# A mixture of experts on one core: each rank gets its own narrow width, six more second products branch, two ranks change the way their second products run

## The chip, the cores and the metric

The kernel runs on one core of a Trainium2 chip. The metric is the device time of one execution in microseconds (us), as the median of several runs. TensorE is called PE here, VectorE DVE, ScalarE ACT, GpSimd POOL and SyncE SP.

## What is computed

Clustered attention over 4 batches, 8 heads and 768 positions makes 3072 tokens of 512 numbers. Then a mixture of experts with 16 experts runs on them. Each token goes to one expert, the best of the best group:

```
for g in range(G):
    ...
    for e in range(Eg):
        ...
        h = np.maximum(xg[mask_e] @ w1[g, e], 0.0)
        ye = h @ w2[g, e]
        combined = g_w[mask_g][mask_e] * e_w[mask_e]
        tok_idx = np.where(mask_g)[0][mask_e]
        out[tok_idx] = combined[:, None] * ye
```

The first products (`@ w1`) take 512 features to 1024, the second ones (`@ w2`) take them back to 512. The change touches only the mixture of experts.

## The kernel before, in words

**Stages.** Attention runs to about 392 us. The first expert and the leftover tokens follow (`part_a`, `bridge`), and from 436 us on the other 15 experts, in falling order of their number of tokens, which the kernel finds at run time. Such a place in the order is called a rank, 0 to 14. A rank has a fixed capacity, the widest it may be: `caps` = 288, 272, 256, 240, 232, 224, 216, 208, 200, 192, 184, 176, 168, 160, 160 tokens. With this input (the reference's own, from its fixed seed) the reference's routing gives the ranks 271, 234, 213, 207, 191, 189, 178, 177, 174, 169, 155, 142, 142, 141 and 133 tokens.

**A round** (`round_`, from L1450). Round k holds the first products of rank k (`up`, L1029) and the second products of rank k-1 (`down`, L1056), taken in turn over eight steps. Every value is carried as a sum of two float16 numbers, a high and a low part, so each product of matrices is made three times (high by high, high by low, low by high).

**First products.** `up` makes 8 accumulations of 12 products (L1044), two accumulations to a step, 96 products of M columns in a rank, M being the rank's capacity or less. Their eviction is one ACT instruction for the high part (`hh`, L1049) and one DVE instruction for the low part (`hl`, L1050) per accumulation.

**Second products, in one of two ways.** By features, `down` makes 4 pieces of 24 products of M columns each (L1078) and evicts each piece by ACT (`yh`, L1084) and DVE (`yl`, L1085). One round on, `settle` turns the result back to tokens with 8 products of 128 columns for each tile of 128 tokens (L1128). By tokens, it makes 24 products of 512 columns for each tile of 128 tokens (L1102), however many tokens the tile has, and no turning back is needed. `feature_major` (L1108) picks the way whose sum of columns is smaller: with M tokens in nt tiles it is by features if 96M + 1024nt < 12288nt. Ranks 2 and 3 go by tokens before the change, the others by features. Either way, each tile's result is scaled by ACT (L1141) and written out by an indirect DMA from POOL's queue (L1142).

**Narrow widths.** `widths` (L1249) compares each rank's count with its capacity and makes a word `wi` with one bit for each rank. `at_width` (L1273) wraps a run of products in a branch on PE: the bit chooses between a body of full width and one that is narrower by `STEP` = 24 columns. The first product of each accumulation has the full width in both bodies. Only the products change, and evictions keep the full width. The first products of all 15 ranks branch; of the second products by features only those of ranks below `CHOSEN` = 9 do. Those in a branch are 24 products in one piece, the others two pieces of 12.

**The stream of weights** (`stream`, L977). Each round brings 8 chunks of 512 KB (`load_chunk`, issued by SP, L818). A chunk's high part is made by ACT (L825) or POOL (L827) in turn, its low part by DVE (L828). These conversions stand at fixed places in the engines' queues between the evictions, since the order of PE, ACT and DVE is that of the program text here (`manual_schedule`). Two sets of weight tiles take turns: rank k+2's weights go into the tiles of rank k. In round 2 the stream has come to the first two chunks of rank 3's second weights by the last steps, and they go into the tiles that rank 1's second products read.

Of the kernel before, what the change touches and what calls it, by code (L numbers as in the profile page):

```python
# [744 lines left out]
class Experts:  # L745
# [11 lines left out]
    TURNED, TURN = (3, 4, 6, 8, 14), 3  # L757
    HI = (0, 1, 0, 1, 0, 1, 0, 1)
    LEAD = 12
    STEP, CHOSEN, BOUND = 24, 9, 15  # L760

    def __init__(self, ctx, tc, R, w1, w2, out, stage, wa):
        self.tc, self.R, self.w1, self.w2, self.out = tc, R, w1, w2, out
# [16 lines left out]
    def setup(self):  # L780
        nc, const, E = self.nc, self.const, self.R.E
        self.io = const.tile([P, E], F32, name="io")
        nc.gpsimd.iota(self.io, [[1, E]], base=0, channel_multiplier=0, allow_small_or_imprecise_dtypes=True)
        self.capr = const.tile([1, E], F32, name="capr")
        i = 0
        while i < E:
            j = i
            while j < E and self.caps[j] == self.caps[i]:
                j += 1
            nc.gpsimd.memset(self.capr[:, i:j], float(self.caps[i]))  # L790
            i = j
        self.four = const.tile([1, E], F32, name="four")
        for r in range(E):
            nc.gpsimd.memset(self.four[:, r:r + 1], float(2 ** r))
        self.word, self.flags = None, {}
        T = self.R.N // self.R.B // P
        self.io16 = const.tile([P, max(self.caps)], F16, name="io16")
        nc.gpsimd.iota(self.io16, [[1, max(self.caps)]], base=0, channel_multiplier=0, allow_small_or_imprecise_dtypes=True)
        self.svals = const.tile([P, T, 3, 2], BF16, name="svals")
        nc.gpsimd.memset(self.svals, 0.0)  # L800
        nc.gpsimd.iota(self.svals[:, :, 0, 0], [[P, T]], base=-P * T, channel_multiplier=0, allow_small_or_imprecise_dtypes=True)
        nc.gpsimd.iota(self.svals[:, :, 1, 0], [[0, T]], base=0, channel_multiplier=1, allow_small_or_imprecise_dtypes=True)
# [251 lines left out]
    def down(self, h, M, W, gcols, idcols, rank=None):  # L1054
# [1 line left out]
        KD, FC, D = R.KD, self.F // P, self.D  # L1056
        w2h, w2l = W
        hh, hl = h
        if self.feature_major(M):

            Mw = self.width(M)
            yh = self.xp.tile([P, KD, Mw], F16, name="yh")
# [42 lines left out]
                    yield  # L1105
            self.emit(py, n, g, idc)

    def feature_major(self, M):  # L1108


        KD, FC, D, nt = self.R.KD, self.F // P, self.D, -(-M // P)
        return 3 * KD * FC * M + 2 * nt * D < 3 * nt * FC * D

# [137 lines left out]
    def widths(self):  # L1251
        nc, E = self.nc, self.R.E
        t = self.small("wt", [1, E, E])
        n = self.small("wn", [1, E])
        a = self.small("wa_", [1, E])
        b = self.small("wb", [1, E])
        w = self.small("ww", [1, 1])
        self.wi = self.small("wi", [1, 1], I32)
        nc.vector.tensor_tensor(out=t, in0=self.pr, in1=self.c17[0:1, 0:E].unsqueeze(1).broadcast_to([1, E, E]), op=ALU.mult)
        nc.vector.tensor_reduce(out=n, in_=t, axis=AX.X, op=ALU.add)  # L1260
        nc.vector.tensor_tensor(out=n, in0=n, in1=self.capr, op=ALU.subtract)
        nc.vector.tensor_scalar(out=a, in0=n, scalar1=-float(self.STEP), scalar2=None, op0=ALU.is_le)
        nc.vector.tensor_tensor(out=b, in0=a, in1=self.four, op=ALU.mult)
        nc.vector.tensor_reduce(out=w, in_=b, axis=AX.X, op=ALU.add)
        nc.vector.tensor_copy(out=self.wi, in_=w)

    def spare(self, k):
        if k not in self.flags:
# [3 lines left out]
    def at_width(self, k, M, body):  # L1272
# [4 lines left out]
        n = self.spare(k)  # L1277

        with self.tc.If(n > 0) as c:
            body(M - self.STEP)  # L1280
        with c.Else():
            body(M)
        self.mm = SimpleNamespace(ins=self.nc.cur_bb.bb.instructions[-1])
# [163 lines left out]
    def ranks(self, bg, state):  # L1447

        E, sizes = self.R.E, self.sizes
        def round_(k, xT, xgs, nxt, down):  # L1450
# [5 lines left out]
            h = []  # L1456
            up = self.up(xT, M, self.weights_of(k, 0), h, k)
            for i in range(8):
                while self.ready < 4 * k + (4 if i >= 4 else 2) or k > 0 and self.ready2 < 4 * k - 4 + (4 if i >= 4 or not self.feature_major(self.caps[k - 1]) else 2):
                    next(self.fill)  # L1460
                next(up, None)
                next(down, None)
# [220 lines left out]
```

## Time and profile before

| what | value |
|---|---|
| median of 3 runs | 717.97 us (717.57 to 720.92) |
| the profiled execution's own time | 720.37 us |
| its span in the profile | 718.5 us |
| PE busy | 691.0 us, 96% |
| DVE busy | 595.7 us, 83% |
| ACT and POOL busy | 477.8 us (66%) and 489.8 us (68%) |
| round 0 begins, the last round ends | 436.36 us, 703.20 us |

The trace gives each instruction's start and duration in the profiled execution. Successive products overlap in PE, so one product's duration is longer than the distance between two starts; the cost of a product is the distance, and the chain of work shows it as the time of 12 or 24 products in a row. Where an instruction has idle time ahead of it, brackets say how much and which instruction ended it. A part of the table of stretches is one round.

### The profile page before, as it was taken

What the parts mean: (1) busy time and instruction counts of PE and PEld (TensorE: products, weight loads), DVE (VectorE), ACT (ScalarE), POOL (GpSimd) and SP (SyncE); (2) the same over time, 40 slices, a digit from 0 to 9 for tenths busy, and PEclk for the clock granted to TensorE, in tenths of its full rate; (3) what the DMA queues carried; (4) which work ended last, traced back from release to release, by engine and by line L of the source; (5) the groups of instructions that cost most, each with busy time, mean ns of one, the idle gap of its engine ahead of it and who ended that gap; (6) DMA issues with size and microseconds to landing.
All of it is one profiled execution on the core that took longest, in us unless ns stands there. A gap on an engine that the chain in (4) does not pass through costs nothing.

```text
span 718.5 us, 25964 instructions
## 1 busy us (share of the span) xinstructions
PE 691.0 (96%) x10520; PEld 587.3 (82%) x10520; DVE 595.7 (83%) x1228; ACT 477.8 (66%) x921; POOL 489.8 (68%) x532
## 2 busy tenths in 40 slices
PE   5989999999999999999998999999999999999996
PEld 3667887887778877888777886889779999999995
DVE  5998989899898998989887747887679798899961
ACT  4558898897988979887995336545445455555542
POOL 9768888899988999989985033545546374574442
PEclk9999999999999999999999999999999999999999
DMA  8865737557485474642746168869879799889931
GB/s 253 196 179 153 204 87 188 134 130 201 83 187 137 123 198 93 131 105 47 193 93 122 61 227 304 280 212 269 310 240 312 253 303 312 268 297 302 291 106 52
DMA packets 91654, 137.23 MB, mean 191 GB/s; under 512 B 43623, under 2 KB 61543, under 8 KB 91512
## 3 DMA queue, kind: packets, MB, share of 16 engines
q1 hardware_dynamic: 85948, 121.81, 60.5%
q0 software_dynamic: 5408, 13.39, 5.5%
q8 instruction: 101, 1.65, 0.9%
q14 instruction: 41, 0.34, 0.1%
q10 hardware_dynamic: 156, 0.03, 0.0%
HBM read 93.25 MB, written 14.10 MB: 149 GB/s over the span
## 4 chain that ended last, share of the span: by engine, by line
PE 64%; DVE 14%; ACT 8%; issue 6%; DMA 4%; POOL 1%; SPq 1%; POOLq 1%; DVEq 0%; ACTq 0%
PE psh L1044 15%; PE psy L1078 12%; PE pso L394 9%; PE psc L320 6%; PE psf L362 5%; PE psf L363 5%; DVE mpart L323 4%; PE psy L1102 4%; ACT p L367 3%; PE psm L253 2%; DVE wl0a L828 1%; PE psm L1128 1%; DMA st<-w 1%; DMA qx<-xbuf,idA 1%; ACT ph L371 1%
## 5 line engine op out<-in xcount | busy, mean ns | idle before, releaser
L374 POOL TENSOR_TENSOR pl<-p 128x512 f16<-128x512 f32 x193 | 198.0, 1050 | 21.0 <-ACT p L367 18.7
L323 DVE TENSOR_REDUCE mpart<-psc 128x1 f32<-128x512 f32 (+1 forms) x282 | 188.6, 682 | 17.4 <-PE psc L320 15.6
L367 ACT ACTIVATE p<-psf 128x512 f32<-128x512 f32 x288 | 171.4, 599 | 41.2 <-PE psf L363 32.1
L394 PE MATMUL pso<-V,pl 128*128 128x65 f16 (+1 forms) x1968 | 160.8, 193 | 0.0
L362 PE MATMUL psf<-A 82*128 82x384 f16 (+2 forms) x576 | 144.1, 275 | 2.3 <-ACT p L367 0.8
L363 PE MATMUL psf<-B 128*128 128x384 f16 (+2 forms) x576 | 143.7, 274 | 0.0
L394 PEld LDWEIGHTS <-pl 128*128 128x128 f16 x1968 | 130.8, 97 | 1.5
L394 PEld LDWEIGHTS <-p 128*128 128x128 bf16 x1632 | 112.6, 98 | 20.4 <-issue 0.8
L394 PE MATMUL pso<-V,p 128*128 128x65 f16 x1632 | 121.0, 193 | 0.0
L374 POOL TENSOR_TENSOR pl<-p,ph 128x512 f16<-128x512 f32 x84 | 96.8, 1161 | 24.5 <-POOL pl L374 9.1
L320 PE MATMUL psc<-A 80*128 80x512 f16 (+1 forms) x376 | 107.8, 332 | 4.0 <-DVE mpart L323 2.4
L1049 ACT ACTIVATE hh<-psh 128x160 f16<-128x160 f32 (+14 forms) x136 | 46.6, 347 | 87.1 <-PE psh L1044 75.7
L1002 POOL DMA_INDIRECT xg<-xbuf,ri x32 | 38.7, 1209 | 85.5 <-PE psm L1012 43.3
L1050 DVE SCALAR_TENSOR_TENSOR hl<-psh,hh 128x160 f16<-128x160 f32 (+14 forms) x136 | 47.5, 369 | 39.1 <-ACT hh L1049 34.6
L363 PEld LDWEIGHTS <-B 128*128 128x128 f16 x576 | 56.9, 99 | 13.8 <-issue 4.1
L1044 PE MATMUL psh<-xT,wh0a 128*128 128x288 f16 (+12 forms) x512 | 66.8, 247 | 0.0
L362 PEld LDWEIGHTS <-A 82*128 82x128 f16 x576 | 56.1, 98 | 9.9 <-issue 1.5
L1044 PE MATMUL psh<-xT,wl0a 128*128 128x288 f16 (+7 forms) x256 | 59.8, 246 | 0.1
L1044 PE MATMUL psh<-xT,wh0b 128*128 128x272 f16 (+6 forms) x448 | 58.7, 247 | 0.5 <-PE psy L1078 0.3
L1044 PE MATMUL psh<-xT,wl0b 128*128 128x248 f16 (+6 forms) x224 | 53.5, 246 | 0.0
L371 ACT CAST ph<-p 128x512 f16<-128x512 f32 x84 | 51.9, 618 | 2.3
L320 PEld LDWEIGHTS <-A 80*128 80x128 f16 x384 | 37.5, 100 | 16.8 <-issue 6.3
(316 smaller groups left out, 1633.2 us busy)
## 6 DMA issues: line engine op xcount, KB each, us to landing
st<-w SPq DMA_DIRECT2D x128, 512.0 KB
B<-parts SPq DMA_DIRECT2D x64, 192.0 KB
kx<-kT SPq DMA_DIRECT2D x16, 384.0 KB
qx<-qT SPq DMA_DIRECT2D x16, 384.0 KB
vx<-vr SPq DMA_DIRECT2D x16, 384.0 KB
A<-parts SPq DMA_DIRECT2D x32, 192.0 KB
xbuf<-xs SPq DMA_DIRECT2D x16, 384.0 KB
A<-mk SPq DMA_DIRECT2D x56, 24.0 KB
```

Of the source, the lines that this page charges most:

```text
L320: last["mm"] = nc.tensor.matmul(out=pc[:, off:off + k1 - k0], lhsT=QA[h % 8][0:80, c * P:(c + 1) * P], rhs=KA[h % 8][0:80, k0:k1], start=T ...
L323: nc.vector.tensor_reduce(out=(mp[:, 0, 0:1], mp[:, :, 1], mp[:, 1, 0:1])[i], in_=pc.rearrange("p (a x) -> p a x", a=n), axis=AX.X, op=ALU ...
L362: nc.tensor.matmul(out=o, lhsT=KA[h % 8][0:82, ks], rhs=QA[h % 8][0:82, q0:q1], start=True, stop=False)
L363: nc.tensor.matmul(out=o, lhsT=KBs[h][:, ks], rhs=QBs[h][:, q0:q1], start=False, stop=True)
L367: cfg["exp"] = nc.scalar.activation(out=p32, in_=pf, func=AF.Exp, scale=QK / (SQ * SQ))
L371: nc.scalar.copy(out=ph, in_=p32)
L374: lo = (nc.vector if u in (EARLY if h < 2 else DVE_LO[h % 8] if h < NH - 2 else DVE_END[h - NH]) else nc.gpsimd).tensor_tensor(out=pl, in0 ...
L394: nc.tensor.matmul(out=O[:, col:col + v.shape[-1]], lhsT=p[:, bs], rhs=v, start=c == 0 and q == 0 and i == 0, stop=c == NCH - 1 and i == l ...
L1044: self.mm = nc.tensor.matmul(out=ph[:, 0:n], lhsT=w[:, k, f * P:(f + 1) * P], rhs=xT[:, a, k, 0:n], start=i == 0, stop=i == 3 * KD - 1)
L1049: nc.scalar.activation(out=hh[:, f], in_=ph[:, 0:M], func=AF.Relu)
L1050: self.ev = nc.vector.scalar_tensor_tensor(out=hl[:, f], in0=ph[:, 0:M], scalar=0.0, in1=hh[:, f], op0=ALU.max, op1=ALU.subtract)
L1078: self.mm = nc.tensor.matmul(out=py[:, 0:n], lhsT=w[:, f, d * P:(d + 1) * P], rhs=a[:, f, 0:n], start=i == 0, stop=i == len(prods) - 1)
```

## The change

The single step `STEP` becomes a table `LESS` with a step for each rank, and `CHOSEN` goes from 9 to 15, so that the second products of ranks 9 to 14 branch too. A row `capn` of 16 narrow widths is written at the start by 16 more small POOL instructions, and `widths` compares the counts with it (one DVE instruction fewer). `feature_major` takes a mean of the full and the narrow width for ranks that branch.

```diff
--- before.py
+++ after.py
@@ -757,7 +757,8 @@
     TURNED, TURN = (3, 4, 6, 8, 14), 3
     HI = (0, 1, 0, 1, 0, 1, 0, 1)
     LEAD = 12
-    STEP, CHOSEN, BOUND = 24, 9, 15
+    CHOSEN, BOUND = 15, 15
+    LESS = 16, 32, 32, 24, 24, 24, 24, 24, 24, 16, 24, 24, 24, 16, 24
 
     def __init__(self, ctx, tc, R, w1, w2, out, stage, wa):
         self.tc, self.R, self.w1, self.w2, self.out = tc, R, w1, w2, out
@@ -789,6 +790,9 @@
                 j += 1
             nc.gpsimd.memset(self.capr[:, i:j], float(self.caps[i]))
             i = j
+        self.capn = const.tile([1, E], F32, name="capn")
+        for r in range(E):
+            nc.gpsimd.memset(self.capn[:, r:r + 1], float(self.narrow(r)))
         self.four = const.tile([1, E], F32, name="four")
         for r in range(E):
             nc.gpsimd.memset(self.four[:, r:r + 1], float(2 ** r))
@@ -1056,7 +1060,7 @@
         KD, FC, D = R.KD, self.F // P, self.D
         w2h, w2l = W
         hh, hl = h
-        if self.feature_major(M):
+        if self.feature_major(M, rank):
 
             Mw = self.width(M)
             yh = self.xp.tile([P, KD, Mw], F16, name="yh")
@@ -1105,9 +1109,11 @@
                     yield
             self.emit(py, n, g, idc)
 
-    def feature_major(self, M):
-
-
+    def feature_major(self, M, rank=None):
+
+
+        if rank is not None and rank < self.CHOSEN:
+            M = (M + self.narrow(rank)) // 2
         KD, FC, D, nt = self.R.KD, self.F // P, self.D, -(-M // P)
         return 3 * KD * FC * M + 2 * nt * D < 3 * nt * FC * D
 
@@ -1258,11 +1264,13 @@
         self.wi = self.small("wi", [1, 1], I32)
         nc.vector.tensor_tensor(out=t, in0=self.pr, in1=self.c17[0:1, 0:E].unsqueeze(1).broadcast_to([1, E, E]), op=ALU.mult)
         nc.vector.tensor_reduce(out=n, in_=t, axis=AX.X, op=ALU.add)
-        nc.vector.tensor_tensor(out=n, in0=n, in1=self.capr, op=ALU.subtract)
-        nc.vector.tensor_scalar(out=a, in0=n, scalar1=-float(self.STEP), scalar2=None, op0=ALU.is_le)
+        nc.vector.tensor_tensor(out=a, in0=n, in1=self.capn, op=ALU.is_le)
         nc.vector.tensor_tensor(out=b, in0=a, in1=self.four, op=ALU.mult)
         nc.vector.tensor_reduce(out=w, in_=b, axis=AX.X, op=ALU.add)
         nc.vector.tensor_copy(out=self.wi, in_=w)
+
+    def narrow(self, k):
+        return self.caps[k] - (self.LESS[k] if k < len(self.LESS) else 0)
 
     def spare(self, k):
         if k not in self.flags:
@@ -1277,7 +1285,7 @@
         n = self.spare(k)
 
         with self.tc.If(n > 0) as c:
-            body(M - self.STEP)
+            body(self.narrow(k))
         with c.Else():
             body(M)
         self.mm = SimpleNamespace(ins=self.nc.cur_bb.bb.instructions[-1])
@@ -1456,7 +1464,7 @@
             h = []
             up = self.up(xT, M, self.weights_of(k, 0), h, k)
             for i in range(8):
-                while self.ready < 4 * k + (4 if i >= 4 else 2) or k > 0 and self.ready2 < 4 * k - 4 + (4 if i >= 4 or not self.feature_major(self.caps[k - 1]) else 2):
+                while self.ready < 4 * k + (4 if i >= 4 else 2) or k > 0 and self.ready2 < 4 * k - 4 + (4 if i >= 4 or not self.feature_major(self.caps[k - 1], k - 1) else 2):
                     next(self.fill)
                 next(up, None)
                 next(down, None)
```

The narrow widths that the counts above choose, before: 288, 248, 232, 216, 208, 200, 192, 184, 176, 192, 160, 152, 144, 160, 136. Ranks 0, 9 and 13 stay at full width there, as their counts are above capacity less 24. With the change: 272, 240, 224, 216, 208, 200, 192, 184, 176, 176, 160, 152, 144, 144, 136. Rank 0 is within its narrow width by one token.

**The way of ranks 1 and 3.** For rank 3 the mean is 228 columns, so 96 x 228 + 2048 = 23936 is below 24576, and its second products go by features. For rank 1 the mean is (272 + 240) / 2 = 256 columns, which is counted as two tiles: 96 x 256 + 2048 = 26624 is not below 24576, and its second products go by tokens, though its capacity of 272 makes three tiles of them (128, 128 and 16 rows).

PE in round 2, where rank 1's second products begin (`wh_9369` and `wh_9386` are the high part of its second weights). Before:

```order
L1279 UNCONDITIONAL_BRANCH
L1279 COMPARE_AND_BRANCH
L1078 LDWEIGHTS wh_9369
L1078 MATMUL psy<-hh,wh_9369 128x272
L1078 LDWEIGHTS wh_9369
L1078 MATMUL psy<-hh,wh_9369 128x248
L1078 LDWEIGHTS wh_9369
L1078 MATMUL psy<-hh,wh_9369 128x248
```

The same place in the change:

```order
L1106 LDWEIGHTS hh
L1106 MATMUL psy<-wh_9386,hh 128x512
L1106 LDWEIGHTS hh
L1106 MATMUL psy<-wl_9387,hh 128x512
L1106 LDWEIGHTS hl
L1106 MATMUL psy<-wh_9386,hl 128x512
```

The branch is gone, and products of 512 columns stand where those of 248 were.

PE at the end of round 2 in the change, where the third tile of rank 1 begins:

```order
L1106 LDWEIGHTS hl
L1106 MATMUL psy<-wh_9386,hl 128x512
L1106 LDWEIGHTS hh
L1106 MATMUL psy<-wh_9386,hh 16x512 [waits Activation_49]
L1106 LDWEIGHTS hh
L1106 MATMUL psy<-wl_9387,hh 16x512 [waits DVE_49]
L1106 LDWEIGHTS hl
L1106 MATMUL psy<-wh_9386,hl 16x512
```

And DVE at that place in the change:

```order
L1054 SCALAR_TENSOR_TENSOR hl<-psh,hh 128x256 [waits Activation_49] x2
L832 SCALAR_TENSOR_TENSOR wl0a<-st,wh0a 128x2x512 [waits DMAHW3_49,Pool_49]
L832 SCALAR_TENSOR_TENSOR wl_9387<-st,wh_9386 128x4x256 [waits DMAHW4_49,Activation_49]
L1287 UNCONDITIONAL_BRANCH
L1054 SCALAR_TENSOR_TENSOR hl<-psh,hh 128x240 [waits Activation_49]
```

The third tile has four more turns than the round has steps, so it stands behind all eight steps. Ahead of it in the program stand the conversions of a chunk of rank 3 into the very tiles that it reads: its first product waits for ACT's part and its second for DVE's. (Rows 256 to 271 hold no token with rank 1's 234.)

PE where rank 10's second products begin. Before:

```order
L1279 UNCONDITIONAL_BRANCH
L1078 LDWEIGHTS wh1b
L1078 MATMUL psy<-hh,wh1b 128x184
L1078 LDWEIGHTS wh1b
L1078 MATMUL psy<-hh,wh1b 128x184
```

The same place in the change:

```order
L1287 UNCONDITIONAL_BRANCH
L1287 COMPARE_AND_BRANCH
L1082 LDWEIGHTS wh1b
L1082 MATMUL psy<-hh,wh1b 128x184
L1082 LDWEIGHTS wh1b
L1082 MATMUL psy<-hh,wh1b 128x160
L1082 LDWEIGHTS wh1b
L1082 MATMUL psy<-hh,wh1b 128x160
```

A branch stands ahead of the piece, and all products behind the first have the narrow width.

## Rows read from the trace of the kernel before

**Rows 1.** The page: busy time by engine, and PE's granted clock in 40 slices.

```profile
PE 691.0 (96%) x10520; PEld 587.3 (82%) x10520; DVE 595.7 (83%) x1228; ACT 477.8 (66%) x921; POOL 489.8 (68%) x532
...
PEclk9999999999999999999999999999999999999999
```

**Rows 2.** PE's waits, 436 to 720 us: total us, times, longest.

```profile
PE psh L1044 <- PE psy L1078: 0.3, 1, 0.3
```

**Rows 3.** Chain of work in order of time: start us, us, what.

```profile
463.61 2.94 PE psy L1078 x24
...
480.84 2.55 PE psy L1078 x24
...
485.79 1.44 PE psm L1128 x24
...
499.79 2.24 PE psh L1044 x24
502.03 2.59 PE psy L1102 x12
...
542.53 2.15 PE psy L1078 x24
...
555.70 0.23 issue
...
563.85 0.89 PE psm L1128 x16
...
645.61 1.90 PE psy L1078 x24
```

**Rows 4.** PE's timeline at ranks 0, 1, 9, 13 and 14: the widths executed.

```profile
436.62 0.29 PE L1044 MATMUL psh<-xT,wl0a 128*128 128x288 f16 x1
...
455.37 0.27 PE L1044 MATMUL psh<-xT,wl0b 128*128 128x248 f16 x1
...
609.23 0.25 PE L1044 MATMUL psh<-xT,wl0b 128*128 128x192 f16 x1
...
674.83 0.23 PE L1044 MATMUL psh<-xT,wl0b 128*128 128x160 f16 x1
...
706.87 0.72 PE L1078 MATMUL psy<-hh,wh1b 128*128 128x160 f16 x8
```

**Rows 5.** DVE's timeline at the end of round 2.

```profile
497.70 0.42 DVE L1050 SCALAR_TENSOR_TENSOR hl<-psh,hh 128x256 f16<-128x256 f32 x1 [0.78 <-ACT hh L1049]
498.04 1.65 DVE L828 SCALAR_TENSOR_TENSOR wl0a<-st,wh0a 128x1024 f16<-128x1024 f32 x1
499.61 2.05 DVE L828 SCALAR_TENSOR_TENSOR wl<-st,wh 128x1024 f16<-128x1024 f32 x1
```

**Rows 6.** DVE's timeline, two conversions of the same size in late rounds.

```profile
657.40 1.21 DVE L828 SCALAR_TENSOR_TENSOR wl0b<-st,wh0b 128x1024 f16<-128x1024 f32 x1
...
670.12 2.36 DVE L828 SCALAR_TENSOR_TENSOR wl1b<-st,wh1b 128x1024 f16<-128x1024 f32 x1
```

**Rows 7.** POOL's timeline beside the second of them.

```profile
670.32 1.08 POOL L827 TENSOR_SCALAR wh0a<-st 128x1024 f16<-128x1024 f32 x1
```

**Rows 8.** Rounds 10 to 12: us, busy PE, PEld, DVE, ACT, POOL; PEclk, DMA share, GB/s.

```profile
626.99:643.85 16.86, 16.72 (x228) 16.23 (x225) 15.96 (x24) 10.12 (x22) 13.32 (x13) 1.00 0.85 290
643.85:659.59 15.74, 15.74 (x226) 15.60 (x225) 15.32 (x23) 9.05 (x21) 8.56 (x9) 1.00 0.92 311
659.59:674.69 15.10, 15.10 (x227) 14.96 (x225) 14.50 (x22) 8.67 (x21) 7.78 (x8) 1.00 0.87 298
```

**Rows 9.** POOL's timeline in the setup, and its first wait behind it.

```profile
22.40 0.60 POOL L794 MEMSET four<- 1x1 f32 x16
...
26.91 1.04 POOL L374 TENSOR_TENSOR pl<-p 128x512 f16<-128x512 f32 x1 [2.89 <-ACT p L367]
```

**Rows 10.** PE's timeline, products of 128 columns in `settle`.

```profile
665.36 0.22 PE L1128 MATMUL psm<-back,yh 128*128 128x128 f16 x1
665.42 0.22 PE L1128 MATMUL psm<-back,yl 128*128 128x128 f16 x1
```

## The prediction, made before the change was run

> **What bounds the kernel now.** I read the page first. It shows PE busy for 691.0 of 718.5 us and its clock at full level in all 40 slices, the upper of its two (2.4 GHz) [rows 1]. Busy PE is not yet bound PE, so next come the waits: from 436 us to the end, which is all that the change touches, one wait of 0.3 us is put down to another instruction [rows 2]. Then the chain of work in order of time, because only there does one see what 24 products cost in a row: through rounds 0 to 14 PE's pieces follow each other with hardly a break [rows 3]. So here the time is PE's sum, and a piece that gets shorter shortens the whole, as long as the engines that feed PE keep up. The table of rounds says where they may not. DVE is busy for 15.96 of 16.86 us in round 10, 15.32 of 15.74 in round 11 and 14.50 of 15.10 in round 12 [rows 8], so it has 0.90, 0.42 and 0.60 us left there.
>
> **The price of a column.** A piece of 24 products takes 2.94 us at 288 columns and 1.90 at 184 [rows 3]. The difference, 1.04 us over 24 x 104 columns, makes 0.417 ns a column. The pieces lie on this line: 24 x 184 x 0.417 ns is 1.84 us, and 1.90 was measured.
>
> **Part 1, the widths.** The timeline shows which width ran: 288 in rank 0, 248 in rank 1, 192 in rank 9, 160 in rank 13, and 160 in rank 14's second products [rows 4]. With the counts, the change narrows these:
> - First products, 88 of 96 of which have the narrow width: ranks 0, 9 and 13 lose 16 columns (1408 each), ranks 1 and 2 lose 8 (704 each). Together 5632 columns, 2.35 us.
> - Second products by features, 92 of 96 narrow: ranks 0, 9 and 13 lose 16 columns (1472 each), ranks 10, 11, 12 and 14 lose 24 (2208 each). Together 13248 columns, 5.52 us.
>
> That is **-7.87 us**. Of it 1.79 us (4288 columns) lies in ranks 0 to 2, and 6.08 us (14592 columns) in ranks 9 to 14. By round, the late part is 0.59 in round 9, 0.61 in 10, 0.92 in 11, 0.92 in 12, 1.51 in 13, 0.61 in 14 and 0.92 behind the last round.
>
> **Part 2, rank 3 by features.** By tokens its 48 products are four times the row of 12 of 512 columns, 4 x 2.59 = 10.36 us. By features they are four pieces of 24, one product at 240 and 23 at 216 columns, as in the row of 2.24 us, and turning back two tiles takes 0.89 [rows 3]: 4 x 2.24 + 0.89 = 9.85. Hence **-0.51 us**.
>
> **Part 3, rank 1 by tokens.** The few words on the change don't name this one, but the order does. By features it costs four pieces of 2.55 and 1.44 for turning back three tiles, 11.64 us. By tokens it costs three tiles of 24 products, the third one for 16 rows, and a product of 512 columns costs the same however few rows come out: 6 x 2.59 = 15.54 us [rows 3]. Hence **+3.90 us**, half of what the widths give.
>
> **Part 4, a new wait at the third tile.** Its second product waits for DVE's conversion of a chunk of rank 3. In the trace of before, the last first products of round 2 end at 497.24 (where the piece of 2.55 ahead of 499.79 begins). DVE then finishes `hl` and makes two conversions, of which the second ends at 499.61 + 2.05 = 501.66 [rows 5], which is 4.42 us later. PE has half a tile left there, 2.59 us, so it would stand for 1.83 us. If both conversions took the 1.21 us of an undisturbed one [rows 6], they would end 0.88 + 2.42 = 3.30 us after the first products, and PE would stand for 0.7. If both took 2.36, it would be 3.0. DVE also loses rank 1's four `yl` in this round, so I take a value between the first two, **+1.3 us**, with bounds of 0 and 3.0. Behind PE's wait stand rank 3's first products, so it delays everything.
>
> **Part 5, DVE in the late rounds.** Rounds 10 to 12 should shorten by 0.61 + 0.92 + 0.92 = 2.45 us, but DVE's work in them stays: evictions keep the full width, and the conversions are the same. Its free time there is 1.92 us. I take the shortfall, **+0.5 us**, with 0 below (buffers let PE run ahead of DVE for a while) and all 2.45 above. The DMA queues would be close too: what round 11 moved at 311 GB/s with a share of 0.92 [rows 8] would fall in 14.82 us instead of 15.74, a share of 0.98.
>
> **Part 6, the branches.** PE gets 28 more branched pieces (rank 3's 4, and 24 in ranks 9 to 14) and loses rank 1's 4. A branch as such shows no cost: the branched piece with 23 products at 208 and one at 232 columns took 2.15 us [rows 3] where the columns alone make 2.09, a surplus of 0.06 like that of the unbranched piece at 184. Once the chain has a gap of 0.23 us at such a piece [rows 3]. I take one, **+0.2 us**, between 0 and 28 x 0.23 = 6.4.
>
> **What costs nothing.** The 16 writes of `capn` on POOL cost what the 16 like them do, 0.60 us, and POOL stands idle for 2.89 us before its first real work [rows 9]. If that cover were gone, they would cost 0.6. One DVE instruction fewer in `widths` lies far from the end. The outputs of rank 1 are three tiles before and after, so ACT's and POOL's work for them stays. Rank 1's four evictions in round 2 go away, and rank 3's four come in round 4.
>
> **The sum.** -7.87 - 0.51 + 3.90 = -4.48 us on PE, and 1.3 + 0.5 + 0.2 = 2.0 of waits: -2.5 us. The durations are those of the profiled execution (720.37 us with a span of 718.5, 2.4 above the median); its rounds are PE's own pieces, so I apply the difference to the median of 717.97: **715.5 us**. The bounds of parts 4 to 6 alone make 713.5 to 725.3; I hold the upper end of part 6 for a case of its own (below).
>
> **Rivals.**
> - *A, the waits hide.* Parts 4 to 6 cost nothing, as PE's own waits were only 0.3 us so far [rows 2]: -4.48, **713.5 us**. Against it: in part 4 even the shortest conversions leave 0.7.
> - *B, DVE holds the late rounds.* A conversion takes 1.21 us, or 2.36 when POOL converts beside it [rows 6, 7]. If this collision comes as often in shorter rounds, rounds 9 to 13 keep their length, as two engines that wait for each other would, and their 4.55 us are lost (0.5 is in the sum): 715.5 + 4.05 = **719.5 us**, slower than before. It decides from where DVE's work exceeds a round's new length on PE: rounds 11 and 12 are past that (15.32 against 14.82, 14.50 against 14.18), round 10 is 0.29 short of it, a quarter of one collision. Against it: a full DVE in one round can be made good in the next, and PE has run beside a DVE as full as in round 11 without waiting.
> - *C, each branch costs.* PE must fetch the code of the body that it jumps to, and each new branched piece shows the gap of 0.23: 28 of them make 6.4 in place of 0.2, **721.7 us**. Against it: the chain shows this gap at one branched piece and not at its neighbours. The Trainium skill has a rule that speaks for C (Runtime: NRT & Kernel Launch, section "Instruction fetch mechanics"): "Branching breaks sequential prefetch", a taken branch to code outside of the fetched window stalls until it is there. The trace agrees at one piece (0.23 us) and disagrees at its neighbours.
> - *D, a rank doesn't narrow.* Rank 0 is within its new width by one token (271 to 272). If its count on the chip came out above, 2880 columns would stay: +1.2, **716.7 us**. The widths executed before agree with the counts in all 15 ranks, so this is unlikely.
> - *E, small products stop shrinking.* If products between 136 and 192 columns cost alike, the 6.08 us of ranks 9 to 14 don't come: **721.6 us**. Against it: products of 128 columns start 55 ns apart [rows 10], and 8 of 160 columns take 0.55 us from one group to the next, 69 ns each. The Trainium skill (TensorE: Matmul & The Clock Gate, section "Back-to-back issue gap") gives sustained spacings of about 81 ns at 128 columns and 131 at 512. By these a column would cost 0.13 ns, and part 1 would give 2.46 us instead of 7.87, as an estimate from that page. The trace has 55 ns at 128 [rows 10] and 2.59 / 12 = 216 ns at 512 [rows 3], so I stay with the rows.
>
> **How the numbers follow.** I give the forecast 0.56 (its own range is 713.6 to 717.4, from the bounds of part 4 and a part of those of part 5), A 0.24, B 0.10, C 0.03, D 0.05 and E 0.02. The range for 8 in 10 reaches from 712.8 (A, with what runs differ by) to 719.5 (B); C, E and the half of B that is above lie outside, and some of A below. A measurement of this kernel can tell about 0.5%, 3.6 us, from no change: faster means under 714.4, slower above 721.6. Three quarters of A and a quarter of the forecast's lower half fall below 714.4, some 0.18 + 0.13; C, half of E and a little of B come out above, 0.07.
>
> **What would show it.** In the profile of the changed kernel, the widths executed should be 272 (rank 0), 240 (1), 224 (2), 176 (9) and 144 (13). Pieces of second products should take 1.67 us in rank 10 (160 columns) where 1.90 stood, and 1.43 in rank 14 (136). Rank 1 should take six rows of about 2.59 us, and PE should wait at the third tile for DVE's conversion, some 1.3 us around the end of round 2, the longest wait behind 436 us. Round 2 should be longer by about 6.3 us (15.54 - 4 x 2.55 - 0.29 + 1.3), round 3 shorter by the 1.44 of turning back, rounds 0 and 1 by 0.6 and 0.9. In rounds 10 to 12 DVE should be busy all the time, and PE idle for some tenths. The prediction is wrong in its main part if round 2 keeps its length, if rank 1's third tile costs far less than 5.2 us, or if late rounds shorten by under half of what part 1 says, with PE waiting for DVE or the chunks.

## The result

The changed kernel takes 725.4 us (median of 6 runs, 724.22 to 729.98) against 717.77 us (6 runs, 717.57 to 720.92) for the kernel before: ratio 1.0127, interval 1.0097 to 1.0158. It is slower by 1.3%, where 0.3% faster was forecast, and it lies outside the range. The profiled execution took 724.22 us with a span of 722.4.

The page of the changed kernel, with the rows that answer to [rows 1] and, of part 3, the queue that carries instructions:

```profile
PE 686.3 (95%) x10536; PEld 581.9 (81%) x10536; DVE 594.1 (82%) x1227; ACT 480.7 (67%) x921; POOL 493.9 (68%) x550
...
PEclk7799999999999999999999999999999999999998
...
q8 instruction: 106, 1.74, 1.0%
```

PE is busy for 4.7 us less than before, and still the time is longer: what PE gained in products it lost idle. The instruction queue had 101 packets (1.65 MB) before and has 106 now. (The two sevens of PEclk lie in the first 36 us, far ahead of what the change touches.)

The waits of PE between 596 and 700 us, where [rows 2] had one of 0.3 us for the whole stretch behind 436 us (columns: us in total, times, longest):

```profile
PE psh L1048 <- issue: 4.7, 4, 2.4
PE psm L1134 <- issue: 0.7, 2, 0.4
PE psy L1082 <- issue: 0.7, 2, 0.4
PE psh L1048 <- DVE hl L1054: 0.3, 1, 0.3
```

6.4 us of waits, 6.1 of them put down to "issue": PE stood still and nothing in the profile, no engine and no transfer, was what it waited for. The chain of work shows them one by one, at round 2 and in rounds 11 to 13 (start us, us, what):

```profile
492.16 1.15 DVE wl L832
493.31 0.04 issue
493.35 5.12 PE psy L1106 x23
498.48 2.35 PE psh L1048 x24
...
656.15 1.67 PE psy L1082 x24
...
660.95 1.10 issue
662.04 1.69 PE psh L1048 x24
...
666.41 0.71 issue
667.12 1.48 PE psh L1048 x21
...
672.12 0.51 issue
...
678.38 1.51 PE psh L1048 x24
...
686.04 1.66 issue
687.70 3.08 PE psh L1048 x24
690.78 1.53 PE psy L1082 x24
```

At 493 us the third tile of rank 1 waits for DVE's conversion, as foreseen. A piece of rank 10's second products takes 1.67 us, as foreseen. New are the pieces of "issue" between products that have all they need. The last of them has a second price. Rounds 2, 9 to 13 and the stretch behind that wait, as a table of stretches (us, busy PE, PEld, DVE, ACT, POOL; PEclk, DMA share, GB/s; rounds 10 to 12 answer to [rows 8]):

```profile
470.92:498.41 27.49, 26.75 (x195) 17.23 (x192) 18.92 (x30) 10.46 (x18) 16.92 (x14) 1.00 0.94 247
...
608.86:625.27 16.41, 16.41 (x228) 16.26 (x226) 13.96 (x22) 9.68 (x20) 9.95 (x11) 1.00 0.92 299
625.27:641.04 15.77, 15.77 (x227) 15.63 (x225) 13.77 (x22) 9.45 (x20) 9.82 (x11) 1.00 0.86 288
641.04:657.66 16.62, 15.52 (x228) 14.60 (x225) 14.57 (x21) 8.49 (x20) 11.24 (x12) 1.00 0.90 305
657.66:674.76 17.10, 14.77 (x228) 14.08 (x226) 15.90 (x25) 9.89 (x21) 7.71 (x9) 1.00 0.93 302
674.76:692.15 17.39, 14.74 (x211) 14.38 (x209) 11.22 (x20) 7.66 (x17) 7.21 (x7) 0.90 0.73 214
...
687.70:690.78 3.08, 3.08 (x27) 3.08 (x28) 0.33 (x1) 0.30 (x1) 0.00 (x0) 0.51 0.05 13
```

Rounds 11 to 13 last 51.11 us where 45.33 us stood (643.85 to 689.18), though their products are shorter. Behind the longest wait the granted clock is 0.51 of full for 3.08 us, the lower level (1.2 GHz), and 24 products that take 1.51 us at the upper one take 3.08. That is 1.6 us more for one wait of 2.4.

**Where the time went, stage by stage.** Both profiles, from the starts of rounds:

| stretch | before | change | difference | forecast |
|---|---|---|---|---|
| up to round 0 | 436.36 | 430.32 | -6.04 | 0 |
| rounds 0 and 1 | 41.92 | 40.60 | -1.32 | -1.5 |
| round 2 | 21.35 | 27.49 | +6.14 | +6.3 |
| rounds 3 to 6 | 75.90 | 73.43 | -2.47 | -2.0 |
| rounds 7 and 8 | 33.53 | 37.02 | +3.49 | 0 |
| rounds 9 to 13 | 80.12 | 83.29 | +3.17 | -3.9 |
| round 14 and the end | 29.32 | 30.25 | +0.93 | -1.5 |

The forecasts are the terms of the prediction set to their rounds (round 3 loses rank 1's 1.44 us of turning back; round 4 loses 10.36 - 8.96 and round 5 gains 0.89; rounds 9 to 13 have -4.55 and 0.7 for parts 5 and 6). The first row is no effect of the change. Over the profiles below, round 0 begins anywhere between 430.1 and 437.7 us, whatever the kernel. From round 0 to the end the two profiles differ by +9.9 us, and the medians by +7.6. Rounds 0 to 6 came out as forecast. All of the error lies behind them.

**The signature.** A wait without a cause in the profile can be one for the instructions themselves. The trace has the packets of the instruction queue: 16 KB each, about 1.1 us long. Beside PE's gaps of 0.4 us or more in rounds 7 to 13 (a gap here is the distance of two products' starts less the first one's columns at 2.4 GHz), with the last packet that began before the gap ended:

```
PE resumes   gap   packet of the instruction queue   resumes behind its end
579.00       1.00  576.39-577.56                      1.44
591.49       1.79  588.60-589.65                      1.84
597.65       0.58  595.28-596.25                      1.40
645.85       0.52  644.73-645.68                      0.17
647.13       0.47  644.73-645.68                      1.45
651.86       0.56  649.08-650.19                      1.67
662.04       1.28  659.49-660.46                      1.58
667.12       0.88  664.66-665.61                      1.51
672.63       0.67  670.23-671.15                      1.48
676.70       0.43  674.14-675.80                      0.90
687.70       2.55  685.05-686.13                      1.57
```

Nine of the eleven end 1.4 to 1.9 us behind the end of a packet, and they make 9.8 of the 10.7 us. Not all of that is a wait without a cause. The profile puts the one at 591.49, where round 8 begins, down to a chunk of weights:

```profile
PE psh L1048 <- DMA st<-w: 1.6, 1, 1.6
```

The chunk landed at 591.23, 0.26 us before PE resumed. In the longest gap the first 0.7 us go to DVE, which ends its `yl` at 686.04. What the chain calls "issue" in the nine adds up to 6.1 us (0.78 + 0.26 + 0.41 + 0.31 + 0.40 + 1.10 + 0.71 + 0.51 + 1.66). Three of the four gaps of 0.3 us or more in the kernel before do so too (PE resumes at 555.93 behind a packet that ends at 554.46, 613.47 behind 611.99, 618.50 behind 617.01), so it was there to be seen. That the queue is PE's is read from its packets, which follow the number of instructions in PE's program: 101 for some 26,500, 106 for some 27,700, and 85 for some 22,100 in the run without any branch below. A branched piece of 24 products has two bodies in the program, 48 instructions of which are never run, and a narrower piece leaves less time in which the next block can come.

Where the gaps stand matters too. Seven of the eleven are at the first product behind a branch or behind a branch's end (591.49, 597.65, 647.13, 651.86, 662.04, 676.70, 687.70), as in the chain above, where "issue" at 660.95 and 686.04 is followed by a whole piece of 24. Four are inside a straight run of products (579.00, 645.85, 667.12, 672.63): "issue" at 666.41 comes three products into a piece.

So a theory F stood against two rivals in the runs: **F**, PE runs out of code; **S**, the third tile of rank 1 stops the stream of weights and the late rounds pay for it; **L**, the late rounds are bound by the supply of weights (DVE or the chunks), whatever PE does.

### The profile page after: what moved, and what is told of

Its sections match the earlier page's. It is cut to its first block, busy times and chain, and to the rows that moved or that the text cites. A ratio compares the mean times of both kernels' runs of the same rounds, so it can differ in the third digit from the quotient of the medians.

```text
span 722.4 us, 26072 instructions
## 1 busy us (share of the span) xinstructions
PE 686.3 (95%) x10536; PEld 581.9 (81%) x10536; DVE 594.1 (82%) x1227; ACT 480.7 (67%) x921; POOL 493.9 (68%) x550
## 3 DMA queue, kind: packets, MB, share of 16 engines
q8 instruction: 106, 1.74, 1.0%
## 4 chain that ended last, share of the span: by engine, by line
PE 61%; DVE 16%; ACT 9%; issue 6%; DMA 5%; POOL 2%; SPq 0%; POOLq 0%; DVEq 0%; ACTq 0%
PE psh L1048 14%; PE psy L1082 10%; PE pso L394 10%; PE psc L320 6%; PE psf L362 5%; PE psf L363 5%; DVE mpart L323 4%; PE psy L1106 3%; ACT p L367 3%; PE psm L253 2%; DMA st<-w 1%; PE psm L1134 1%; DVE wl L832 1%; ACT ph L371 1%; DVE wl0a L832 1%
## 5 line engine op out<-in xcount | busy, mean ns | idle before, releaser
L1006 POOL DMA_INDIRECT xg<-xbuf,ri x32 | 41.5, 1298 | 92.1 <-PE psm L1016 46.4
L1048 PE MATMUL psh<-xT,wh0a 128*128 128x272 f16 (+14 forms) x512 | 65.9, 246 | 3.4 <-issue 1.8
L1048 PE MATMUL psh<-xT,wl0a 128*128 128x272 f16 (+7 forms) x256 | 59.5, 245 | 0.5 <-issue 0.5
L1048 PE MATMUL psh<-xT,wl0b 128*128 128x240 f16 (+6 forms) x224 | 53.4, 248 | 0.0
L1148 POOL DMA_INDIRECT out_dram<-y,ri x32 | 39.2, 1225 | 19.8 <-ACT y L1147 12.8
```

What stands on the lines that cost most here:

```text
L1048: self.mm = nc.tensor.matmul(out=ph[:, 0:n], lhsT=w[:, k, f * P:(f + 1) * P], rhs=xT[:, a, k, 0:n], start=i == 0, stop=i == 3 * KD - 1)
```

## The experiments

All ratios are to the kernel before on the same chip, with 95% intervals. Chips differ (the kernel before had medians of 716.6 to 722.2 us), so ratios are compared, not times.

### First: which half of the change costs the time

**Rank 1 by features, the rest of the change kept.**

```diff
     def feature_major(self, M, rank=None):
+        nt = -(-M // P)
         if rank is not None and rank < self.CHOSEN:
             M = (M + self.narrow(rank)) // 2
-        KD, FC, D, nt = self.R.KD, self.F // P, self.D, -(-M // P)
+        KD, FC, D = self.R.KD, self.F // P, self.D
```

> The tiles of a rank are counted from its full width again, so rank 1's second products go by features (narrow, 240 columns); the rest of the change stays. Theory S (the third tile of rank 1 stops the stream of weights for some 6 us, and the late rounds pay for it): the 3.9 us of products and the wait at the third tile go, and PE's gaps in rounds 7 to 13, more than 10 us with the lower clock behind them, shrink to under 4 us: 713 to 716.5 us, below the kernel before. Rival L (the late rounds are bound by the supply of weights whatever rank 1 does): the gaps of rounds 9 to 13 stay as large as their savings, and the time is 717 to 719. Rival C (each new branch costs): only the 4.8 us of the tile go: about 720.5.

Measured: 723.85 us against 720.68, ratio 1.0028 (1.0000 to 1.0056). Rank 1 by tokens thus costs about 1.0127 - 1.0028 = 0.99%, 7 us, and without it the change is still no gain. The gaps stay: between 596 and 700 us its waits put down to "issue" are 4.8 us (1.5 + 1.3 + 1.1 + 0.9). S is refuted for the late rounds, since no tile stands behind anything here. Taken against the 717.8 us that they assumed, S expected a ratio below 0.999, L up to 1.002 and C, the branches, 1.004: L's upper end and C lie in the interval.

**The second products of ranks 9 to 14 unbranched, rank 1 by tokens.**

```diff
-    CHOSEN, BOUND = 15, 15
+    CHOSEN, BOUND = 9, 15
```

> Second products of ranks 9 to 14 don't branch (full width), everything else as in the change, rank 1 by tokens too. Theory S and rival L: those ranks' second products get 4.9 us longer (11776 columns at 0.417 ns), but PE's gaps there get shorter by about as much, so 724 to 727 us. Rival C: the branches' stalls go, some 10 us, against 4.9 us of products: about 720.

Measured: ratio 1.0026 (1.0003 to 1.0050). The other half taken out gives as much, 1.01%. With 4.9 us more of products this kernel is some 7 us faster than the change. That is what the rival of the branches expected (720, or 1.003), and neither S nor L.

**The kernel before with rank 1 by tokens alone.**

```diff
-        return 3 * KD * FC * M + 2 * nt * D < 3 * nt * FC * D
+        return M != self.caps[1] and 3 * KD * FC * M + 2 * nt * D < 3 * nt * FC * D
```

> The kernel before with one thing of the change alone: rank 1's second products by tokens. Sum on PE alone (no hold-up of the stream): 717.8 + 3.9 + 1 = 722.7 us, with no new gaps behind round 3. Theory S: DVE idles some 6 us at the end of round 2, and the late rounds, which have little room in the kernel before, pay part of it again: 724 to 728 us, with PE gaps in rounds 7 to 13. Rival L: 722.7, as late rounds are no faster than before.

Measured: ratio 1.0109 (1.0065 to 1.0154), 7.8 us. That is in S's range and above the 4.9 us of the sum on PE, but for reasons that S didn't have. PE's waits between 480 and 520 us:

```profile
PE psy L1102 <- DVE wl L828: 3.6, 1, 3.6
PE psy L1102 <- ACT wh L825: 0.3, 1, 0.3
```

The wait at the third tile itself was 3.9 us here, where the change shows 0.74. Behind it PE ran at the lower level of its clock (granted 0.50 from 503.10 to 506.51 us), which the change doesn't show at that place. Round 2 took 32.34 us, 11.0 more than in the kernel before, and round 3 was 1.5 shorter. The rounds behind it are as long as before (rounds 10 to 14 differ by at most 0.01 us from those of the kernel before), so next to nothing is paid later (0.5 us in round 8 and 0.6 at the end). The wait's length differs from kernel to kernel, and it can be more than the 3.0 us that the prediction gave as a bound.

**Rank 1 by tokens, its turns spread over the eight steps.**

```diff
-                if f % 2 == 1:
+                if (t * FC + f) % 3 == 2 if len(gcols) == 3 else f % 2 == 1:
                     yield
```

> Rank 1's second products by tokens, but the 24 turns of its three tiles are spread over the round's eight steps (three to a step in place of two), so that no tile stands behind the conversions of rank 3's chunks; the rest as in the change. Theory S: the 3.9 us of products stay, the wait at the third tile and DVE's idle time of 6.8 us there go, and so do most late gaps: 717 to 720 us, some 4 above the run with rank 1 by features. Rivals L and C: only the wait goes, 724 to 725.

Measured: ratio 1.0092 (1.0058 to 1.0127). Against the change that is 0.35% less with intervals that overlap, about what the wait alone was to give, and not the 6 to 8 us of S. PE has no wait at rank 1's tiles any more, and its gaps in rounds 7 to 13 are as large as in the change (1.92, 1.15, 1.01, 1.77 and 2.69 us are the largest; the profile puts the first down to a chunk of weights and the second to DVE's `hl`). S fell with this.

### Second: code against width

Four kernels in which only ranks 9 to 14's second products differ, all with rank 1 by features: branched or not, narrow or wide. The branched narrow one is the first run above.

**Narrow without a branch** (the wide bodies of ranks 9 to 14 are left out):

```diff
-                    self.at_width(rank if two else None, M, products)
+                    if two and rank >= 9:
+                        products(self.narrow(rank))
+                    else:
+                        self.at_width(rank if two else None, M, products)
```

> As the run with rank 1 by features, but the second products of ranks 9 to 14 are narrow without a branch (the wide body is left out; it is never taken with this input). The same products, some 1220 fewer instructions in PE's program. Theory F (PE runs out of code: most gaps end about 1.5 us after a 16 KB fetch of its code has ended, and the untaken bodies double the code of each piece): the gaps of rounds 9 to 13, 7 to 8 us there, fall to under 2, and the time falls by 6 to 8 us against that run, below the kernel before by 0.8 to 1.2%. Rival L (the late rounds wait for weights): the same time as that run within 1 us.

Measured: 711.6 us against 716.57, ratio 0.9937 (0.9913 to 0.9962). The same products as in the run at 1.0028, in the same order on PE, and 0.91% faster, 6.5 us, through 24 branches and 1224 instructions fewer. (Against the kernel before it is 0.6%, a little less than the 0.8 expected.)

**Branched, both bodies wide.**

```diff
-                    self.at_width(rank if two else None, M, products)
+                    self.at_width(rank if two else None, M, (lambda m: products(M)) if two and rank >= 9 else products)
```

> As the run with rank 1 by features, but both bodies of the second products of ranks 9 to 14 have the full width: the code of the change without its narrowing. Theory F: 4.9 us more of products, while the code is as long, so gaps remain (3 to 6 us, each ending about 1.5 us after a fetch): equal to that run or up to 3 us slower, and 3 us or more slower than the run with the same products unbranched. Rival L: the gaps vanish as products are longer, and the time equals the unbranched run's.

Measured: ratio 1.0067 (1.0038 to 1.0096). PE's waits between 596 and 700 us:

```profile
PE psy L1082 <- issue: 3.8, 3, 1.7
PE psm L1135 <- issue: 1.2, 1, 1.2
```

**Wide without a branch.**

```diff
-                    self.at_width(rank if two else None, M, products)
+                    self.at_width(rank if two and rank < 9 else None, M, products)
```

> As the run with rank 1 by features, but the second products of ranks 9 to 14 are wide without a branch (pieces of 24 in one step, as there). Theory F: 4.9 us more of products and some 7 us fewer of gaps than the run with rank 1 by features: 2 to 4 us faster than it, at or below the kernel before (by 0 to 0.5%). Rival L: the same as the run with rank 1 by features, within 1 us.

Measured: ratio 0.9961 (0.9936 to 0.9985), 0.67% (4.8 us) below the first run, where F had 2 to 4 us. Its waits in the same stretch:

```profile
PE psy L1082 <- issue: 1.5, 1, 1.5
```

The four together:

| ranks 9 to 14 | branched | not branched | price of the branches |
|---|---|---|---|
| narrow | 1.0028 | 0.9937 | 0.91%, 6.5 us |
| wide | 1.0067 | 0.9961 | 1.06%, 7.6 us |
| gain of narrowing | 0.39% | 0.24% | |

A branch with a second body that is never run costs 6.5 to 7.6 us on 24 pieces (each to about 2.7 us, from the intervals), and it does so where it saves nothing at all. From round 0 to the end the profiles give 5.2 us (281.8 against 276.6) for the narrow pair and 6.1 (287.9 against 281.8) for the wide one. Not all of it is code: 1.5 us is a wait for ACT behind the last round that only the kernels with late branches have (below). L is refuted for rounds 9 to 13: without the branch they do get shorter, 75.0 us in the narrow pair's profiles where the branched one takes 81.7. Narrowing alone gives 1.7 to 2.8 us in the medians where 4.9 us of products go; between the two unbranched profiles it gives 5.2 (276.6 against 281.8), so what the medians lack stays open. In these profiles the narrow one has two late gaps behind a fetch, 0.62 and 1.45 us, against one of 1.66 in the wide one. The branch and the second body always come and go together here, so the four kernels don't tell which of the two costs the time.

**No branch at any product** (all wide bodies are left out):

```diff
     def at_width(self, k, M, body):
...
-        n = self.spare(k)
-
-        with self.tc.If(n > 0) as c:
-            body(self.narrow(k))
-        with c.Else():
-            body(M)
-        self.mm = SimpleNamespace(ins=self.nc.cur_bb.bb.instructions[-1])
+        body(self.narrow(k))
```

> As the run with rank 1 by features, but no product branches: all have the narrow width that is taken anyway with this input (the wide bodies are left out), some 5900 instructions fewer in PE's program. Theory F: not one gap in rounds 0 to 13 that ends 1.5 us after a code fetch; 0.5 to 2 us faster than with the late second products alone unbranched, 1 to 1.5% below the kernel before. Rival L: gaps of the same size remain, with waits for conversions or chunks, and the time is that of the run with rank 1 by features.

Measured: 705.87 us against 716.57, ratio 0.9863 (0.9835 to 0.9890), 9.8 us. Against the run with the late pieces alone unbranched that is 0.74%, 5.3 us, more than twice what F had expected, and about what the five gaps of 0.3 us or more in that run's rounds 7 to 13 add up to (5.0; one of them, 1.00 at 586.97, is put down to DVE's conversion). It is the price of the other 92 branched pieces, 0.06 us each where the last 24 cost 0.3. The instruction queue has 85 packets, and PE has no gap of 0.15 us or more from round 0 to 13. Rounds 11 and 12 of its table of stretches:

```profile
630.94:645.77 14.83, 14.83 (x228) 14.69 (x226) 14.83 (x23) 9.37 (x20) 10.79 (x10) 1.00 0.87 298
645.77:659.98 14.21, 14.21 (x228) 14.07 (x226) 14.21 (x26) 9.06 (x20) 8.66 (x8) 1.00 0.91 314
```

PE and DVE are both busy without a pause, and the rounds are 0.91 and 0.89 us shorter than in [rows 8], where part 1 gave 0.92 each. Here the sum on PE came true to a few hundredths, with the full DVE beside it.

### Third: one part alone, and what can be kept

**The kernel before with the branches of ranks 9 to 14 alone.**

```diff
-    STEP, CHOSEN, BOUND = 24, 9, 15
+    STEP, CHOSEN, BOUND = 24, 15, 15
```

> The kernel before with one part of the change alone: the second products of ranks 9 to 14 branch (CHOSEN 15 with the one step of 24; ranks 10, 11, 12 and 14 narrow, 9 and 13 do not fit). PE has 3.7 us fewer products (8832 columns) and some 1220 more instructions. Theory F: gaps of 5 to 8 us that end about 1.5 us after a code fetch eat it and more: 0.2 to 0.8% slower than before. Rival L: the same as before within 0.2%, with waits for DVE or chunks; a branch that costs nothing: 0.5% faster.

Measured: ratio 1.0079 (1.0048 to 1.0109), at the upper end of F's expectation. PE's waits between 596 and 700 us:

```profile
PE psh L1044 <- issue: 3.8, 2, 2.0
PE psy L1078 <- issue: 3.0, 2, 1.5
PE psm L1128 <- issue: 1.9, 2, 1.0
PE psh L1044 <- PE psy L1078: 0.4, 1, 0.4
PE psh L1044 <- DVE yl L1085: 0.4, 1, 0.4
```

8.7 us of "issue" where the kernel before has none in this view, through one constant.

**The change without its two losses.** Rank 1 by features as in the first run, and `CHOSEN` = 9.

> The change with its two losses taken out and its branches otherwise as they were: rank 1 by features, and second products of ranks 9 to 14 unbranched and wide in two pieces of 12, as before the change. Left are the steps by rank (ranks 0 to 2, first products of 9 and 13) and rank 3 by features. PE's sum is 2.96 us (7104 columns) + 0.51 below the kernel before. Theory F: the code is 330 instructions longer than before (rank 3's second body), so gaps stay as small as before or grow a little where blocks end elsewhere: 0.2 to 0.5% faster than before. Rival L: the same as before within 0.2%.

Measured: ratio 0.9956 (0.9931 to 0.9982). What is left of the change, the steps by rank and rank 3 by features, gives 3.2 us, close to its sum of 3.5. The wide run without a late branch (0.9961) has the same work in pieces of 24 and comes out alike, so the size of the piece is not what costs.

**The narrow widths as capacities, no branch.**

```diff
-    LESS = 16, 32, 32, 24, 24, 24, 24, 24, 24, 16, 24, 24, 24, 16, 24
+    LESS = ()
...
-        self.caps = [288, 272, 256, 240, 232, 224, 216, 208, 200, 192, 184, 176, 168, 160, 160, self.CA]
+        self.caps = [272, 240, 224, 216, 208, 200, 192, 184, 176, 176, 160, 152, 144, 144, 136, self.CA]
```

(beside the edits of the run without any branch)

> A version meant to beat both and to hold for every input: the narrow widths become the capacities themselves (272, 240, 224, ..., 136), so there is no branch and no second body, and a rank with more tokens than that leaves them to the loop for the rest, which the kernel has anyway. Evictions, gathers and the first product of each accumulation are narrow too. Theory F: no gap after a code fetch in rounds 0 to 13; PE has about 1.5 us less than in the run without any branch (first products of the accumulations) and 1 us less in rank 1 (two tiles by tokens): 1.5 to 2.2% below the kernel before. Rival L (DVE or the chunks, now the next bound): no more than in the run without any branch, 1.0 to 1.4%.

Measured: 708.96 us against 722.16, ratio 0.9810 (0.9786 to 0.9834). It beats both kernels, by 1.9% and, over the ratios, 3.1%. (What an input with more tokens in a rank would cost here was not measured.) Its code takes 84 packets, and no gap of rounds 2 to 13 follows a fetch as above. The waits that it has between 596 and 700 us are others:

```profile
PE psh L1048 <- DVE hl L1054: 1.7, 2, 1.1
```

With the code out of the way DVE is the next bound, in round 12, the mechanism of rival B.

## Why the prediction was wrong

**Bound, and the price of a column: right.** PE's sum bounds the rounds, and a column costs 0.417 ns down to 136. The pieces of ranks 0 to 14 in the change have the forecast lengths (1.67 us in rank 10, and 24 products of 144 columns at 1.51). Rival E, a floor under narrow products, fell with that. Rival D fell too, as rank 0 ran at 272 columns.

**Parts 1 to 3: right.** The widths, rank 3 by features and rank 1 by tokens made -4.48 us. The columns of all products from round 0 on, at 2.4 GHz, sum up to 262.1 us before and 257.7 now: -4.4. In the run without any branch the whole of part 1 arrived.

**Part 4, the third tile: right mechanism, a size that varies.** The wait was 0.74 us in the change, and +1.3 was taken. Round 2 grew by 6.14 us (6.3 forecast), in part by luck: the wait was 0.56 us shorter than taken and the products 0.35 longer. The bound of 3.0 was too low: the kernel before with this part alone had 3.9. By the medians, rank 1 by tokens costs 7.1 to 7.8 us (first and third run) where parts 3 and 4 had 5.2, so some 2 us of the miss may lie here, which is within what the intervals leave open. Rival A fell, since the wait did show.

**Part 5, DVE in the late rounds: too dear here.** With 0.5 taken, the run without any branch shows 0: DVE was busy all through rounds 11 and 12, and PE waited for nothing. The prediction had taken DVE's busy time as fixed work. It is not: it fell from 15.32 to 14.83 us in round 11 with the length of the round. Between 596 and 700 us PE's waits for DVE's `hl` are 0.3 us in the change; only at the narrow capacities do they come to 1.7.

**Part 6, the branches: the step that failed.** "I take one, +0.2 us, between 0 and 28 x 0.23 = 6.4." Measured: 6.5 to 7.6 us for the 24 pieces of ranks 9 to 14 alone, at the bound or above it. The prediction priced the branch as the same small gap at each piece, found most pieces free, and took the gap at 555.70 us for a stray. That gap isn't even at the branch, for five products of the piece stand ahead of it in the chain of the kernel before:

```profile
555.24 0.46 PE psy L1078 x5
```

What a branch costs falls at few places, and not always at the branch. The untaken bodies lengthen the code, and PE stands still until some 1.5 us behind the end of a packet of it. Of the nine gaps of the change that end so, six stand behind a branch or its end and three in a straight run. So gaps are rare and large (0.4 to 2.5 us) rather than frequent and small. Rival C, fetching the code of the body that PE jumps to, was nearest in mechanism and in time (721.7 us, slower), but got 0.03, since it was tested against the wrong pattern: "the chain shows this gap at one branched piece and not at its neighbours" is what a supply in blocks looks like. Two further costs of the branched pieces had no step. After the longest gap the clock was at its lower level and 24 products took 1.6 us longer. And at the end, rank 14's branched pieces changed what PE stands behind: in the change, in the first run, in the spread and the branched wide ones and in the kernel before with late branches, PE waits 1.5 us for ACT's `yh` between rank 14's second and third piece, and in none of the unbranched kernels. The 0.92 us saved behind the last round went into that. With some 2 us of part 4 this makes some 8 to 9.5 of the 10.1 us between the forecast (-2.5) and the medians (+7.6).

The Trainium skill (Runtime: NRT & Kernel Launch, section "Instruction fetch mechanics") says that an engine's code comes in 16 KiB blocks, that the cost of crossing a block is mostly hidden, and that branching breaks the prefetch. The runs agree on the size of a block (106 packets for 1.74 MB). The run without any branch agrees with "mostly hidden" (85 packets, and no gap of 0.15 us or more from round 0 to 13), and the branched ones agree with the rule on branches where a gap is behind one (1.10 us of "issue" at 660.95). Inside a straight run of a branched kernel the crossing wasn't hidden (0.71 us at 666.41).

**Still open.** The runs show that branches with an untaken body cost this time and that most gaps end behind a fetch. They don't separate the length of the code from the jumps: no run has the one without the other. They don't show what starts a fetch, why one block is late and the next is not, or why rounds 7 and 8 have gaps in some profiles (3.5 us more in the change, 1.6 of it put down to a chunk of weights) and not in others with the same code up to there (the unbranched run with rank 1 by tokens). So for the start of round 8 theory L isn't refuted. That the DMA engines, busy for 0.9 of the time with weights, delay the fetches is only argued; it wasn't tried.

## What to carry to other kernels

Price a run-time branch by what it does to the engine's supply of code, not by its own instructions: count the instructions of the program, never-run bodies too, against the time that they run for, above all where products are short, and look for PE waits on "issue" that end behind a packet of the instruction queue. A narrower body saves columns times 0.417 ns; a branch with a second body that is never run cost 0.27 to 0.32 us per piece of 24 products in ranks 9 to 14, about the 23 x 24 columns (0.23 us) that it was to save, and 0.06 us per piece in the mean of the 92 others. And where a rule chooses between two ways by a mean of sizes, count its tiles from the size that runs: 16 rows beyond 256 cost rank 1 a whole tile and 1% of the kernel.

## What the runs showed of the hardware that was not expected

- A queue whose packets follow the length of PE's program brings 16 KB at a time, about 1.1 us each, and in rounds 9 to 14 of the change one every 5 us. Nine of PE's eleven gaps in rounds 7 to 13 ended 1.4 to 1.9 us after the end of such a packet.
- Behind a wait of 2.4 us with PE idle, in round 13 of the change, the granted clock was 0.51 for 3.08 us. Rounds 11 and 12, with waits of up to 1.1 us, show 1.00. The run with rank 1's turns spread had 2.5 us idle at the same product (690.78) and shows 1.00 behind it.
- DVE's busy time is no fixed amount: 23 instructions of round 11 took 15.32 us in a round of 15.74, and 23 took 14.83 in one of 14.83, with PE waiting in neither.
